# A spectral filter split into pieces between the steps of an FFN, forward and backward, in one kernel

## The chip, the cores and the metric

One core of a Trainium2 chip runs the whole program. The metric is the device time of one execution in microseconds (us). Ratios between kernels use runs that alternated on one chip. The kernel before has a median of 1678.64 us over the runs taken beside the changed one.

Names used below: PE multiplies matrices; PEld loads its weights; DVE, ACT and POOL are the vector, scalar and general-purpose engines; SP here only issues DMAs (its rows are marked SPq). L12 is line 12 of the kernel that the view is of.

## The reference, cut to what matters

The kernel computes a gated mix of a spectral filter and a GEGLU feed-forward network, and all seven gradients.

```python
def _A_ref(x, w_r, w_i):                      # x: 1 x 2048 x 576, bfloat16
    X = rfft2(x.astype(float32)) * (w_r + 1j * w_i)
    return irfft2(X, s=(S, D)).astype(bfloat16)

def _B_ref(x, w_gate, w_up, w_down):          # F = 4608
    return (gelu_tanh(x @ w_gate) * (x @ w_up)) @ w_down

g = sigmoid((x * gate_w).sum(-1, keepdims=True))
out = g * _A_ref(x) + (1 - g) * _B_ref(x)
# outputs: out, then by jax.vjp for grad_out: dx, dw_r, dw_i, dw_gate, dw_up, dw_down, dgate_w
```

## The kernel before

Five parts run one after another: setup (transposes of x, gate, sine and cosine tables); the spectral part as matmuls with those tables; the FFN's hidden layer in 18 groups of 8 steps, in which the last group's weight gradients are worked off between the steps of the next; and a final stage in two halves (down projection and gate, then dx), which reads the hidden activations back transposed by DMA.

The spectral part, one of its forward pieces. Of three evictions (`evac`) two go to ACT and one to DVE, from three PSUM buffers (`ps`):

```python
def fwd_D_S1_t(self, xT_t, t, scr):
    yps = self.ps.tile([P, 2, 512], F32, tag="specps")
    for c in range(2):
        for ci in range(5):
            nc.tensor.matmul(yps[:, c, :DF], lhsT=xT_t(ci), rhs=tb.Dfwd[:, ci, c, :], ...)
    Y = self.rot.tile([P, 2, DF], BF16, tag="specY")
    evac(nc, Y[:], yps[:, :, :DF])
    # ... four matmuls with R into vps, evac to V
    self.st.dma_start(scr[:, t, :, :], V[:])          # read back later with another layout
```

The gradient is scaled by 1 - g and transposed on PE:

```python
ident = res.tile([P, P], BF16, name="ident")
make_identity(nc, ident[:])                           # POOL
...                                                   # tables, whole spectral part
for t in range(T):
    # dB = don1 * omg32, DVE and ACT in turn
transpose_to_dchunks(nc, pst1, ident, lambda ci, t: dB[:, t, ...], dBT, T)
```

The FFN's step and its order:

```python
def H(g, tp):
    for w, xt in ((wg_g, xT), (wu_g, xT), (wdT_g, dBT)):
        # 10 matmuls of 256 columns into one PSUM bank
    # ... ACT: q, xb, hu, s (sigmoid), sq (square), da (copy);  DVE: 12 instructions
    for k, tl in enumerate((A, dHg, dHu)):
        LD.dma_start(scr[k][tp][:, :, fsl]..., tl[:])  # SP stores

for g in range(NG):                                    # 18
    for tp in range(NT):                               # 8
        H(g, tp)
        for _ in range(quota[tp]):
            if pend: pend.pop(0)()                     # weight-gradient work of group g-1
    pend = W_units(g)
```

The boundary to the final stage:

```python
for f0 in range(0, NFC, 12):
    LD.dma_start(wd_all[:, f0:f0 + 12, :], wd_v[:, f0:f0 + 12, :])
for u in pend: u()                                     # last weight gradients
...
ensure(6)                                              # first six transposed loads ("pin")
for t in range(T):                                     # first half: 72 matmuls of 288 columns per t
    ...
    if 1 <= t < 1 + len(wT_loads):                     # gate AND up weights, transposed, 12 loads
        LD.dma_start_transpose(...)
```

Of the kernel before, what the change touches and what calls it, by code (L numbers as in the profile page):

```python
# [9 lines left out]
ACT = mybir.ActivationFunctionType  # L10
# [18 lines left out]
A_GELU = 0.044715  # L29


def centered_mod(nc, pool, X, N, tagp=""):
    shp = list(X.shape)
    y = pool.tile(shp, F32, tag=tagp + "cm_y")
    nc.scalar.activation(y[:], X, ACT.Identity, scale=1.0 / N, bias=MAGIC)  # L35
    nc.scalar.activation(y[:], y[:], ACT.Identity, scale=1.0, bias=-MAGIC)  # L36
    r = pool.tile(shp, F32, tag=tagp + "cm_r")
    nc.vector.scalar_tensor_tensor(r[:], y[:], -float(N), X, op0=ALU.mult, op1=ALU.add)
    ar = pool.tile(shp, F32, tag=tagp + "cm_ar")
    nc.vector.scalar_tensor_tensor(ar[:], r[:], -1.0, r[:], op0=ALU.mult, op1=ALU.max)  # L40
    return r, ar


def trig(nc, r, ar, N, halfpi, cos_out=None, sin_out=None, nsin_out=None):
    s = 2.0 * math.pi / N
    if cos_out is not None:
        nc.scalar.activation(cos_out, ar, ACT.Sin, bias=halfpi, scale=-s)
    if sin_out is not None:
        nc.scalar.activation(sin_out, r, ACT.Sin, scale=s * EPS_SCALE)
    if nsin_out is not None:  # L50
        nc.scalar.activation(nsin_out, r, ACT.Sin, scale=-s * EPS_SCALE)
# [6 lines left out]
def build_tables(nc, tc, const_pool):  # L58
    tb = Tables()
    with tc.tile_pool(name="tbtmp", bufs=1) as tmp:  # L60
        halfpi = const_pool.tile([P, 1], F32, name="halfpi")
        nc.vector.memset(halfpi[:], math.pi / 2)
        tb.halfpi = halfpi
        lrow = tmp.tile([P, DF], F32, tag="lrow")
        nc.gpsimd.iota(lrow[:], pattern=[[1, DF]], base=0, channel_multiplier=0, allow_small_or_imprecise_dtypes=True)
        dcol = tmp.tile([P, 5], F32, tag="dcol")
        nc.gpsimd.iota(dcol[:, 0:4], pattern=[[128, 4]], base=0, channel_multiplier=1, allow_small_or_imprecise_dtypes=True)
        nc.gpsimd.iota(dcol[:, 4:5], pattern=[[0, 1]], base=DCH[4][0], channel_multiplier=1, allow_small_or_imprecise_dtypes=True)
        lcol = tmp.tile([P, 3], F32, tag="lcol")
        nc.gpsimd.iota(lcol[:, 0:2], pattern=[[128, 2]], base=0, channel_multiplier=1, allow_small_or_imprecise_dtypes=True)  # L70
        nc.gpsimd.iota(lcol[:, 2:3], pattern=[[0, 1]], base=LCH[2][0], channel_multiplier=1, allow_small_or_imprecise_dtypes=True)
        krow = tmp.tile([P, P], F32, tag="krow")
        nc.gpsimd.iota(krow[:], pattern=[[1, P]], base=0, channel_multiplier=0, allow_small_or_imprecise_dtypes=True)
        scol = tmp.tile([P, T], F32, tag="scol")
        nc.gpsimd.iota(scol[:], pattern=[[1, T]], base=0, channel_multiplier=16, allow_small_or_imprecise_dtypes=True)
        drow = tmp.tile([P, D], F32, tag="drow")
        nc.gpsimd.iota(drow[:], pattern=[[1, D]], base=0, channel_multiplier=0, allow_small_or_imprecise_dtypes=True)
        mrow_i = tmp.tile([P, P], I32, tag="mrow_i")
        nc.gpsimd.iota(mrow_i[:], pattern=[[1, P]], base=0, channel_multiplier=0)
        qcol_i = tmp.tile([P, 1], I32, tag="qcol_i")  # L80
        nc.gpsimd.iota(qcol_i[:], pattern=[[0, 1]], base=0, channel_multiplier=1)

        XD = tmp.tile([P, 5, DF], F32, tag="XD")
        for c in range(5):
            nc.vector.tensor_scalar(XD[:, c, :], lrow[:], dcol[:, c:c + 1], None, op0=ALU.mult)
        r, ar = centered_mod(nc, tmp, XD[:], D, "D")
        Dfwd = const_pool.tile([P, 5, 2, DF], BF16, name="Dfwd")
        trig(nc, r[:], ar[:], D, halfpi[:], cos_out=Dfwd[:, :, 0, :], nsin_out=Dfwd[:, :, 1, :])
        tb.Dfwd = Dfwd
        XR = tmp.tile([P, T, P], F32, tag="XR")  # L90
        for t in range(T):
            nc.vector.tensor_scalar(XR[:, t, :], krow[:], scol[:, t:t + 1], None, op0=ALU.mult)
        r, ar = centered_mod(nc, tmp, XR[:], S, "R")
        R = const_pool.tile([P, T, 3, P], BF16, name="Rtab")
        trig(nc, r[:], ar[:], S, halfpi[:], cos_out=R[:, :, 0, :], nsin_out=R[:, :, 1, :], sin_out=R[:, :, 2, :])
        tb.R = R
        k2row_i = tmp.tile([P, P], I32, tag="k2row_i")
        nc.vector.tensor_single_scalar(k2row_i[:], mrow_i[:], 3, op=ALU.arith_shift_right)
        jrow_i = tmp.tile([P, P], I32, tag="jrow_i")
        nc.vector.tensor_single_scalar(jrow_i[:], mrow_i[:], 7, op=ALU.bitwise_and)  # L100
        tcol_i = tmp.tile([P, 1], I32, tag="tcol_i")
        nc.vector.tensor_single_scalar(tcol_i[:], qcol_i[:], 3, op=ALU.arith_shift_right)
        jcol_i = tmp.tile([P, 1], I32, tag="jcol_i")
        nc.vector.tensor_single_scalar(jcol_i[:], qcol_i[:], 7, op=ALU.bitwise_and)
        k2row = tmp.tile([P, P], F32, tag="k2row")
        nc.vector.tensor_copy(k2row[:], k2row_i[:])
        jrow = tmp.tile([P, P], F32, tag="jrow")
        nc.vector.tensor_copy(jrow[:], jrow_i[:])
        tcol = tmp.tile([P, 1], F32, tag="tcol")
        nc.vector.tensor_copy(tcol[:], tcol_i[:])  # L110
        jcol = tmp.tile([P, 1], F32, tag="jcol")
        nc.vector.tensor_copy(jcol[:], jcol_i[:])
        XB = tmp.tile([P, P], F32, tag="XB")
        nc.vector.tensor_scalar(XB[:], k2row[:], tcol[:, 0:1], None, op0=ALU.mult)
        mask = tmp.tile([P, P], F32, tag="maskB")
        nc.vector.tensor_scalar(mask[:], jrow[:], jcol[:, 0:1], None, op0=ALU.is_equal)
        r, ar = centered_mod(nc, tmp, XB[:], 16, "B")
        Btmp = tmp.tile([P, 3, P], F32, tag="Btmp")
        trig(nc, r[:], ar[:], 16, halfpi[:], nsin_out=Btmp[:, 0, :], cos_out=Btmp[:, 1, :], sin_out=Btmp[:, 2, :])
        B = const_pool.tile([P, 3, P], BF16, name="Btab")  # L120
        for v in range(3):
            nc.vector.tensor_tensor(B[:, v, :], Btmp[:, v, :], mask[:], op=ALU.mult)
        tb.B = B
        XA = tmp.tile([P, 3, D], F32, tag="XA")
        for c in range(3):
            nc.vector.tensor_scalar(XA[:, c, :], drow[:], lcol[:, c:c + 1], None, op0=ALU.mult)
        r, ar = centered_mod(nc, tmp, XA[:], D, "A")
        Atmp = tmp.tile([P, 3, 2, D], F32, tag="Atmp")
        trig(nc, r[:], ar[:], D, halfpi[:], cos_out=Atmp[:, :, 0, :], nsin_out=Atmp[:, :, 1, :])
        clcol = tmp.tile([P, 3], F32, tag="clcol")  # L130
        sd = 1.0 / (S * D)
        m1 = tmp.tile([P, 3], F32, tag="m1")
        nc.vector.tensor_scalar(m1[:], lcol[:], 0.0, -sd, op0=ALU.is_equal, op1=ALU.mult)
        m2 = tmp.tile([P, 3], F32, tag="m2")
        nc.vector.tensor_scalar(m2[:], lcol[:], float(DF - 1), -sd, op0=ALU.is_equal, op1=ALU.mult)
        nc.vector.memset(clcol[:], 2.0 * sd)
        m3 = tmp.tile([P, 1], F32, tag="m3")
        nc.vector.tensor_scalar(m3[:], lcol[:, 2:3], 256.0, 2.0 * sd, op0=ALU.is_ge, op1=ALU.mult)
        nc.vector.tensor_copy(clcol[:, 2:3], m3[:])
        nc.vector.tensor_tensor(clcol[:], clcol[:], m1[:], op=ALU.add)  # L140
        nc.vector.tensor_tensor(clcol[:], clcol[:], m2[:], op=ALU.add)
        Ainv = const_pool.tile([P, 3, 2, D], BF16, name="Ainv")
        for c in range(3):
            nc.vector.tensor_scalar(Ainv[:, c, :, :], Atmp[:, c, :, :], clcol[:, c:c + 1], None, op0=ALU.mult)
        tb.Ainv = Ainv
        ucol = tmp.tile([P, 3], F32, tag="ucol")
        nc.vector.memset(ucol[:], 1.0)
        m4 = tmp.tile([P, 1], F32, tag="m4")
        nc.vector.tensor_scalar(m4[:], lcol[:, 2:3], 256.0, None, op0=ALU.is_ge)
        nc.vector.tensor_copy(ucol[:, 2:3], m4[:])  # L150
        Ainv_u = const_pool.tile([P, 3, 2, D], BF16, name="Ainv_u")
# [8 lines left out]
    return tb  # L160


_evac_ctr = [0]


def evac(nc, out, in_, eng=None):
# [595 lines left out]
```

## Time and profile before

| | before |
|---|---|
| time, median of 4 runs | 1678.64 us (1677.68 to 1680.4) |
| span of the profiled run, granted clock | 1676.1 us, 0.98 |
| first FFN step | 299 us |
| FFN after the first group, to the last weight gradient | 339.7 to 1206.9: 867 us |
| idle PE at the boundary | 5.6 us |
| final stage, halves | 170 and 293 us |

The page gives an engine's busy share first, and then tenths of busy time in 40 slices of 42 us:

```profile
PE 1540.7 (92%) x13440; PEld 1280.9 (76%) x13440; DVE 863.7 (52%) x2162; ACT 709.3 (42%) x1226; POOL 83.8 (5%) x171
...
PE   2777678899999999999999999999898889999998
PEclk9998888999999999999999999999999999999999
```

Eight slices at the left where PE is not full, then twenty where it is, then a final stage a little below. At the boundary SP's queue is short:

```profile
1184.36 6.09 SPq L614 DMA_DIRECT2D wd_all<-in_B_w_down_dram  x3
1190.56 6.25 SPq L563 DMA_DIRECT2D out_dram<-dwd  x2
...
1208.07 9.29 SPq L640 DMA_TRANSPOSE pin<-scr  x5
```

The columns are start, duration, engine, line, operation and count. The down weights are asked for at 1184, the stores of the last weight gradients follow, and the transposed loads start 1.2 us after PE has finished, at 1208.

### The profile page before, as it was taken

The page shows a single profiled execution, that of the slowest core. Times are in us where ns is not written, and L with a number is a line of the kernel's source. Part 1 is how long each engine was busy: PE and PEld are TensorE (multiplying, and loading weights), DVE is VectorE, ACT ScalarE, POOL GpSimd, SP SyncE. Part 2 cuts the span into 40 slices and gives each one's busy share as a digit, 9 for nine tenths or more (in the row PEclk, how much of TensorE's full clock was granted, in tenths as well). Part 3 has the DMA queues.
Part 4 walks back from the last instruction along what each step waited for, and adds up shares of the span by engine and source line. Part 5 has one row for each costly group of instructions (what it writes and reads, how often), then busy time and mean ns, then how long its engine had stood idle before and what let it go on. Part 6 is the DMA issues. An engine that isn't in the chain of part 4 may idle for free.

```text
span 1676.1 us, 33316 instructions
## 1 busy us (share of the span) xinstructions
PE 1540.7 (92%) x13440; PEld 1280.9 (76%) x13440; DVE 863.7 (52%) x2162; ACT 709.3 (42%) x1226; POOL 83.8 (5%) x171
## 2 busy tenths in 40 slices
PE   2777678899999999999999999999898889999998
PEld 2554455788888888888888888888776667777776
DVE  6127520787777777777777777777222221001001
ACT  7554446666665556565556565556100000000000
POOL 1122231000000000000000000000000000000000
PEclk9998888999999999999999999999999999999999
DMA  3244564243332443432343342333699998877773
GB/s 117 103 110 114 152 173 134 61 120 104 105 102 83 109 108 105 108 98 84 104 109 107 109 101 85 101 106 86 201 207 226 210 214 170 157 147 154 151 150 85
DMA packets 490395, 212.42 MB, mean 127 GB/s; under 512 B 306560, under 2 KB 484608, under 8 KB 489728
## 3 DMA queue, kind: packets, MB, share of 16 engines
q1 hardware_dynamic: 483424, 189.01, 49.1%
q0 software_dynamic: 6816, 21.28, 3.7%
q8 instruction: 105, 1.72, 0.4%
q14 instruction: 50, 0.41, 0.1%
HBM read 43.25 MB, written 93.82 MB: 82 GB/s over the span
## 4 chain that ended last, share of the span: by engine, by line
issue 87%; PE 6%; ACT 2%; POOL 2%; DMA 1%; DVE 1%; SPq 0%; POOLq 0%; ACTq 0%
PE yps L202 2%; PE yps L269 1%; ACT Y L171 1%; DMA wg_g<-in_B_w_gate_dram 1%; POOL scr_p L246 1%; POOL out_dram L685 1%; POOL dxa_scr L282 1%; DMA xn<-in_A_x_dram 0%; POOL out_dram L731 0%; PE vps L208 0%; PE zps L254 0%; SPq L221 0%; PE zps L256 0%; ACT y L36 0%; ACT y L35 0%
## 5 line engine op out<-in xcount | busy, mean ns | idle before, releaser
L502 PEld LDWEIGHTS <-xT 128*128 128x128 bf16 x2880 | 281.8, 98 | 42.6 <-issue 8.7
L718 PEld LDWEIGHTS <-pin 128*128 128x128 bf16 x2304 | 225.4, 98 | 56.8
L571 PEld LDWEIGHTS <-xn 128*128 128x128 bf16 x2304 | 224.0, 98 | 29.7 <-issue 3.6
L502 PE MATMUL hps<-wu_g,xT 128*128 128x256 bf16 x1440 | 180.7, 273 | 7.1 <-ACT da L520 7.0
L502 PE MATMUL hps<-wg_g,xT 128*128 128x256 bf16 x1440 | 180.7, 273 | 0.4 <-ACT dBT L171 0.4
L502 PE MATMUL hps<-wdT_g,dBT 128*128 128x256 bf16 x1440 | 180.7, 273 | 0.0
L672 PE MATMUL bps<-wd_all,pin 128*128 128x288 bf16 x1152 | 151.2, 296 | 24.7 <-DMA pin<-scr 24.7
L672 PEld LDWEIGHTS <-pin 128*128 128x128 bf16 x1152 | 115.5, 101 | 60.4 <-DMA pin<-scr 28.0
L502 PEld LDWEIGHTS <-dBT 128*128 128x128 bf16 x1440 | 140.9, 98 | 16.3
L555 PE MATMUL wps<-dB,A 128*128 128x288 bf16 x1152 | 152.4, 286 | 0.0
L511 ACT ACTIVATE q<-hps 128x512 bf16<-128x512 f32 x144 | 86.1, 598 | 153.8 <-PE hps L502 152.4
L718 PE MATMUL xps<-wgT_all,pin 128*128 128x288 bf16 x1152 | 149.0, 286 | 0.0
L718 PE MATMUL xps<-wuT_all,pin 128*128 128x288 bf16 x1152 | 149.0, 286 | 0.0
L728 DVE SCALAR_TENSOR_TENSOR f32t<-gwf,dlog,f32t 128x576 f32<-128x576 f32 x16 | 13.1, 817 | 240.5 <-ACT f32t L726 240.5
L555 PEld LDWEIGHTS <-A 128*128 128x128 bf16 x1152 | 112.7, 98 | 26.6
L571 PE MATMUL wps<-dHu,xn 128*128 128x256 bf16 x1152 | 131.7, 273 | 0.0
L571 PE MATMUL wps<-dHg,xn 128*128 128x256 bf16 x1152 | 131.5, 273 | 0.0
L518 ACT ACTIVATE s<-s 128x512 bf16<-128x512 bf16 x144 | 90.9, 631 | 92.0 <-DVE s L514 92.0
L726 ACT COPY f32t<-xps 128x576 f32<-128x576 f32 x16 | 10.2, 640 | 275.9 <-PE xps L718 275.9
L519 ACT ACTIVATE sq<-s,nhalf 128x512 bf16<-128x512 bf16 x144 | 104.0, 722 | 4.7
L513 DVE TENSOR_SCALAR s<-q 128x512 bf16<-128x512 bf16 x144 | 41.6, 289 | 113.9 <-ACT q L511 113.9
L517 ACT CAST hu<-hps 128x512 bf16<-128x512 f32 x144 | 84.7, 588 | 2.1
(200 smaller groups left out, 1885.0 us busy)
## 6 DMA issues: line engine op xcount, KB each, us to landing
scr<-A SPq DMA_DIRECT2D x144, 128.0 KB, 1.8
scr<-dHg SPq DMA_DIRECT2D x144, 128.0 KB, 1.9
scr<-dHu SPq DMA_DIRECT2D x144, 128.0 KB, 1.9
out_dram<-dw SPq DMA_DIRECT2D x72, 128.0 KB, 1.8
out_dram<-dwd SPq DMA_DIRECT2D x36, 144.0 KB, 1.9
wd_all<-in_B_w_down_dram SPq DMA_DIRECT2D x3, 1728.0 KB, 13.2
scr_p<-V POOLq DMA_DIRECT2D x32, 144.5 KB, 2.5
Vp<-scr_p SPq DMA_DIRECT2D x16, 289.0 KB, 7.1
```

The lines of the kernel that those rows point to most:

```text
L171: nc.scalar.copy(out, in_)
L202: nc.tensor.matmul(yps[:, c, :DF], lhsT=xT_t(ci), rhs=tb.Dfwd[:, ci, c, :], start=(ci == 0), stop=(ci == 4))
L502: nc.tensor.matmul(pt[:, tt, :], lhsT=xt[:, ci, tp * TPB + tt, :], rhs=w[:, ci, :], start=(ci == 0), stop=(ci == 4))
L511: nc.scalar.activation(q[:], hg[:], ACT.Square)
L513: V.tensor_scalar(s[:], q[:], A_GELU, 1.0, op0=ALU.mult, op1=ALU.add)
L517: nc.scalar.copy(hu[:], hu_ps[:])
L518: nc.scalar.activation(s[:], s[:], ACT.Sigmoid, scale=2.0 * C_GELU)
L519: nc.scalar.activation(sq[:], s[:], ACT.Square, bias=nhalf[:])
L555: nc.tensor.matmul(wps[:, :288], lhsT=tl(0, t)[:, fch * P:(fch + 1) * P], rhs=dB[:, t, h * 288:(h + 1) * 288], start=(t == 0), stop=(t == ...
L571: nc.tensor.matmul(wps[:, cc, :], lhsT=xn[:, t, (c0 + cc) * P:(c0 + cc + 1) * P], rhs=tl(k, t), start=(t == 0), stop=(t == T - 1))
L672: nc.tensor.matmul(bps[:, h, :288], lhsT=At[:, r, :], rhs=wd_all[:, fc, h * 288:(h + 1) * 288], start=(fc == 0), stop=(fc == NFC - 1))
L718: nc.tensor.matmul(xps[:, h, :288], lhsT=src[:, r, :], rhs=wT[:, fc, h * 288:(h + 1) * 288], start=(n < 2), stop=(n >= 4 * NFC - 2))
```

## The change

Its intent is to fill PE from the start: the spectral part no longer runs ahead of the FFN but is cut into 192 pieces (201 slots, with gaps), which are emitted between the FFN's steps; every order is set by hand. To reach the FFN sooner, the gradient is transposed by DMA instead of by PE, and the scaling by 1 - g moves behind the matmul (`da`). The transposed gate weights become a loop of 18 loads ahead of the final stage. ACT loses two instructions of a step and gains a second sigmoid; DVE takes over the eviction of `da`. To make room, the FFN's buffers shrink: its steps get 4 PSUM banks instead of 5, its weight gradients 2 instead of 3, and its element-wise and staging tiles two buffers instead of three.

```diff
-        with tc.tile_pool(name="pA", bufs=1) as pA, ...:      # the whole spectral part, 4 phases
-            ...
+    for t in range(T):
+        load_dOT(t)                       # two DMA transposes on SP, straight from DRAM
+        if t % 4 == 3:
+            nc.gpsimd.memset(dOT[0:D4NEW, 4, t - 3:t + 1, :], 0.0)
+            LD.dma_start(dB[:, t - 3:t + 1, :], do_v[:, t - 3:t + 1, :])
+    ...
+    ident = res.tile([P, P], BF16, name="ident")
+    make_identity(nc, ident[:])
+    tb = iotas(nc, res, unit)             # POOL
     ...
-        nc.scalar.activation(sq[:], s[:], ACT.Square, bias=nhalf[:])
-        nc.scalar.copy(da[:], da_ps[:])
+        nc.scalar.activation(om[:], s[:], ACT.Sigmoid, scale=-2.0 * C_GELU)
+        V.tensor_tensor(da[:], da_ps[:], omg32[:, t0:t0 + TPB].unsqueeze(2).to_broadcast([P, TPB, FG]), op=ALU.mult)
     ...
+    def pftile():
+        return pf.tile([P, 2, 512], F32, tag="pf", name="pf")   # one buffer of two banks
+    ...                                   # forward, middle and inverse pieces, all evicted by ACT
+        for p in range(T // 2):           # middle
+            if p > 0:
+                out.append(pre(p))        # loads Vp (two), Wt (two) for this pair
+            out += [s2(p, "x", 0), s2(p, "x", 1), s2(p, "g", 0), s2(p, "g", 1)]
+            ...
+            out += [s1(p, "m1", 0, scr_p1), s1(p, "m1", 1, scr_p1)]
     for g in range(NG):
         for tp in range(NT):
-            H(g, tp)
+            fft_until(want(step, 0))      # pieces that are due
+            pts = H_mm(g, tp)
+            tiles = H_ew1(g, tp, pts)
+            fft_until(want(step, 1))
+            H_ew2(g, tp, tiles)
             ...
+    wgT_all = []
+    for f0 in range(0, NFC, 2):
+        u = unit([2, D], name="wgT")
+        LD.dma_start_transpose(u[:], B_w_gate[:, f0 * P:(f0 + 2) * P])
     wd_all = ...                          # loads, weight gradients, final stage as before
```

## The prediction

> **What bounds the kernel now.** I first cut the run at the program's own stages with the view of busy time by stretch, cuts from the order-of-time view: spectral part and setup, first FFN group (18 groups of 8 steps), other groups, last weight-gradient work, and the two halves of the final stage.
>
> ```profile
> 0.00:298.90 298.90, 202.45 (x1600) 147.58 (x1601) 115.41 (x206) 163.40 (x249) 65.94 (x138) 0.93 0.44 127
> 298.90:339.70 40.80, 33.67 (x300) 29.27 (x300) 35.17 (x98) 27.87 (x51) 0.00 (x0) 1.00 0.26 72
> 339.70:1183.00 843.30, 843.30 (x7831) 739.77 (x7830) 635.25 (x1709) 495.24 (x889) 0.00 (x0) 1.00 0.38 101
> 1183.00:1211.70 28.70, 23.91 (x226) 20.24 (x223) 3.46 (x7) 2.34 (x5) 0.00 (x0) 0.96 0.80 247
> 1211.70:1382.60 170.90, 150.97 (x1152) 115.51 (x1153) 44.33 (x105) 9.59 (x15) 8.14 (x15) 0.95 1.13 213
> 1382.60:1676.00 293.40, 286.43 (x2339) 228.56 (x2336) 30.10 (x41) 10.88 (x17) 9.76 (x18) 1.00 0.75 145
> ```
>
> Columns: stretch, length, busy us of PE, weight load, DVE, ACT, POOL, then granted clock, DMA share, GB/s. From 340 to 1183 PE never idles at clock 1.00, DVE 75%, ACT 59%. In the first 299 us no engine is full: a chain of stages. From 1212 to 1383 the DMA share is over 1. The list of waits says what PE waited for:
>
> ```profile
> PE bps L672 <- DMA pin<-scr: 24.7, 11, 5.6
> PE zps L254 <- DMA wg_g<-in_B_w_gate_dram: 13.1, 1, 13.1
> PE vps L208 <- ACT Y L171: 12.1, 18, 0.8
> PE tp L184 <- ACT xT L171: 11.9, 4, 9.5
> PE zps L254 <- DMA Vp<-scr_p: 11.6, 1, 11.6
> ```
>
> The first is the final stage's transposed loads; the rest are spectral. Busy PE overstates: the starts in order of time give PE's true pace.
>
> ```profile
> 602.10 1.25 PE L502 MATMUL hps<-wg_g,xT 128*128 128x256 bf16 x10
> 603.19 1.25 PE L502 MATMUL hps<-wu_g,xT 128*128 128x256 bf16 x10
> 604.28 1.25 PE L502 MATMUL hps<-wdT_g,dBT 128*128 128x256 bf16 x10
> 605.38 2.12 PE L555 MATMUL wps<-dB,A 128*128 128x288 bf16 x16
> 607.34 3.66 PE L571 MATMUL wps<-dHg,xn 128*128 128x256 bf16 x32
> 610.83 1.25 PE L502 MATMUL hps<-wg_g,xT 128*128 128x256 bf16 x10
> ```
>
> A step's 30 matmuls take 3.28 us (109 ns each at 256 columns), a dwd piece 1.96 (122.5 ns at 288), a dw piece 3.49. A group is 8x3.28 + 4x1.96 + 4x3.49 + 1.9 (tail) = 49.9 us, without a gap.
>
> **What the Trainium skill says.** "VectorE: DVE Perf Modes", The perf-mode tier table: tensor_tensor runs 2x from bf16 SBUF and 1x with a PSUM operand. The trace agrees (groups by shape, FFN stretch and, last, spectral stretch; the numbers after the bar are total us and ns of one):
>
> ```profile
> L514 DVE TENSOR_TENSOR s<-xb,s 128x512 bf16<-128x512 bf16 x127 | 54.0, 425 | 18.4 <-ACT xb L512 11.7
> ...
> L513 DVE TENSOR_SCALAR s<-q 128x512 bf16<-128x512 bf16 x127 | 36.7, 289 | 105.8 <-ACT q L511 105.8
> ...
> L234 DVE TENSOR_TENSOR Gspec<-xps,srow 128x578 bf16<-128x578 f32 x16 | 11.3, 753 | 1.0 <-PE xps L230 1.0
> ```
>
> "DMA: Bandwidth & Descriptors", DMA Transpose (X-bar): the plain DMA transpose comes from Sync or Scalar only; so the new ones lengthen SP's queue, where each cost 1.2 to 1.9 us of issue in this trace. Same page, Two DMAs through the same engine are not ordered: a DMA reading what another wrote must wait for its completion; Vp loads after scr stores show it (11.6 us above). "TensorE: Matmul & The Clock Gate", opening table: DVE and ACT are strict FIFO, so spectral pieces placed behind FFN work wait for it. This trace's fixed order is consistent, but does not isolate it.
>
> **The change part by part.** Times are from the span's start.
>
> (1) Removed: the separate spectral stage, 298.9 us. What must remain on PE is its matmuls: forward 32x(10+4) and middle 64x4 at 124 ns, inverse 32x(6 at 109 + 12 at 122.5 ns) = 55.7 + 32 + 67.8 = 155 us. They enter a PE without gaps, so all but some 6 us in the first group's gaps are paid: 150.
>
> (2) New setup. DVE now builds all tables in small float32 pieces before the first step. With this trace's durations (0.48 per 128x289 scaling, 150 + n/0.96 ns for the scalar-tensor form, 0.2 to 0.5 otherwise): D 9, x's evictions 3.4, R 13.5, B 4, A 9, started at 3.5, so 43; sigmoid and table load 3; 16 dB scalings 5. On SP, 32 gradient transposes at about 1.2 (wdT's small ones take 1.22 to 1.29) are 39 after 10 us of loads; the last dB load lands near 53. Both agree: the first step's DVE work starts at 54, not 299.
>
> (3) First group, DVE-bound before (35.2 of 40.8). DVE per step after: 9 tensor_tensor x 0.425 + 3 tensor_scalar x 0.287 + da from PSUM 0.69 (753 scaled to 512) = 5.4; queued instructions overlap about 6% (the same sum before gives 40.0 per group against 37.5 busy), so 5.06. Eight make 40.5: group done at 94.5.
>
> (4) Groups to the end of weight gradients: before 1211.7 - 339.7 = 872, PE-paced, unchanged. Plus 150.
>
> (5) Stalls from interleaving. Program order, which I counted, puts 201 slots (192 pieces) on 135 steps. DVE per group: 8x5.06 plus evictions 1.6 = 42 of 60 us: fine in the forward and inverse part. In the middle (5.6 groups) products add per pair 6x0.76 + 6x0.46 + 0.3 = 7.6 us, 1.49 pairs per group, so 52.5 of 56 us. There DVE paces the first four steps of a group (6.5 us against PE's 5.7), and each pair's Vp load is issued immediately before its use, behind the previous step's stores. A step's DVE work ends about 7.4 to 8 us after its first matmul, plus issue and landing about 3 = 10.9. The eight first uses fall where PE arrives at about 10, 11, 5.7, 3.8, 11, 5.2, 6.6, 11: waits 1+1+6+7+1+6+4+1 = 27. With product waits 6 and DVE pacing elsewhere 7: 40. The single two-bank PSUM buffer costs about 0.7 at each group with no weight work between two pieces: 5.
>
> (6) Final stage. 5.3 MB of gate-weight transposes leave the DMA-bound half (36.6 MB in 171 us, 213 GB/s): 31.3 MB takes 147, near PE's 1152x0.1225 = 141, so 146. But they now precede wd_all and the first pin loads on SP: 18 at about 1.6 = 29 us, then wd_all issue 6, output stores 5, pin 2 + 4.3 landing = 46, against 28 us of remaining weight work: a new wait of 17. Second half unchanged: 293.4.
>
> Sum: 94.5 + 872 + 150 + 45 + 17 + 146 + 293 = 1617.5; add 1.8 of time over span: 1619. Shares of (5) and (6) may hide in each other's slack, and an ordering this deliberate suggests fewer waits than worst case; I lower it by 9: **1610 us**, 4% faster.
>
> **Rivals.**
> A, nearly all waits vanish: PE is in order but DVE catches up in heavy weight-work steps, and SP runs ahead. For it: no PE wait in 843 us now. Then (5) is about 10 and (6) about 5: about 1565.
> B, DVE becomes the bound: if broadcast products miss the 2x rate they take 1.35 us, DVE needs about 58 of 56 us in the middle, and every Vt and Y eviction sits behind a sigmoid that waits for DVE. Against: the present odd-offset products already take 0.76. It would give 1650.
> C, DMA contention and SP's blocking order delay weight loads: FFN DMA share is 0.38 and the spectral traffic adds little; against, except at the boundary. Time 1630 to 1650.
>
> **Range and chances.** A and B bracket the range: 1560 to 1655. Two per cent is 1645; only B or C in full reach it. Faster 0.83, same 0.15, slower 0.02.
>
> **What would show it.** Right: first FFN step's DVE work near 54; a PE without gaps in forward and inverse groups, its length near 60 us per group; in the middle groups PE waits on Vp loads and products of 30 to 45 us in all; DVE near 94% there; a wait of 10 to 20 us between the last weight gradient and the first bps matmul; bps half near 146. Wrong: a first step after 65, PE waits spread over all groups, DVE full outside the middle, product instructions near 1.35 us, or no wait at the boundary.

## The result, and the profile after

The changed kernel is correct and slower: 1730.95 us (1728.73 to 1733.01, 4 runs) against 1678.64 us. The ratio is 1.031, 95% interval 1.0292 to 1.0328. A ratio is the mean time of one kernel's runs over that of the other's of the same rounds, so it isn't quite the ratio of the medians. The profiled run's span is 1729.0 us at clock 0.962.

The page of after, to set against the one of before:

```profile
PE 1519.5 (88%) x13280; PEld 1275.0 (74%) x13280; DVE 907.1 (52%) x2295; ACT 624.3 (36%) x1093; POOL 25.7 (1%) x55
...
PE   0339999999987797898999999999929999999998
PEclk9869999999998999999999999999969999999999
```

Three holes appear: nothing on PE in the first slice and little in the next two; dips to 7 and 8 between the 12th slice and the 19th; and a slice at 2 of 10 near the end. The view of busy time by stretch, cut at the stages of after (columns as in the prediction), gives their lengths:

```profile
0.00:57.70 57.70, 0.00 (x0) 0.10 (x1) 0.06 (x1) 1.28 (x1) 2.76 (x11) 1.00 0.55 138
57.70:109.80 52.10, 19.45 (x220) 17.38 (x220) 42.95 (x109) 24.08 (x43) 4.99 (x12) 0.67 0.13 30
109.80:161.20 51.40, 40.43 (x316) 32.90 (x316) 44.35 (x122) 30.76 (x55) 0.00 (x0) 0.90 0.27 75
161.20:455.90 294.70, 293.04 (x2664) 252.59 (x2662) 200.54 (x523) 158.44 (x281) 0.00 (x0) 1.00 0.37 100
455.90:830.00 374.10, 318.69 (x2776) 268.49 (x2775) 277.95 (x706) 179.06 (x319) 0.00 (x0) 0.94 0.42 113
...
1256.00:1290.50 34.50, 0.00 (x1) 0.01 (x1) 1.06 (x2) 0.58 (x1) 0.00 (x0) 0.55 0.93 246
1290.50:1435.90 145.40, 143.23 (x1153) 113.24 (x1154) 44.88 (x105) 9.57 (x15) 8.26 (x15) 0.99 1.14 215
1435.90:1729.00 293.10, 286.30 (x2338) 228.45 (x2335) 30.10 (x41) 10.85 (x17) 9.72 (x18) 1.00 0.73 144
```

The first 57.7 us hold almost nothing on any engine. The forward groups (161 to 456) are full, as the prediction has it. In the middle (456 to 830) DVE is at 278 of 374 us, 74%, and PE is not full either: nobody is the bound, they wait. Then comes a hole of 34.5 us. Both halves of the final stage are what was predicted.

The list of PE's waits (line, what for, total us, times, longest):

```profile
PE tp L259 <- POOL ident masks.py:199: 57.7, 1, 57.7
PE pf L475 <- DMA Vp<-scr_x: 44.4, 8, 11.4
PE acc L739 <- DMA pin<-scr: 36.7, 4, 34.5
...
PE pf L412 <- ACT Y L416: 6.0, 1, 6.0
```

**The first hole.** POOL, in order of time; the bracket gives the idle time before and what ended it:

```profile
23.87 0.52 POOL L232 MEMSET dOT<- 64x512 bf16 x1 [23.41 <-DMA dOT<-in_grad_out_dram]
34.94 0.52 POOL L232 MEMSET dOT<- 64x512 bf16 x1 [10.56 <-DMA dOT<-in_grad_out_dram]
46.07 0.52 POOL L232 MEMSET dOT<- 64x512 bf16 x1 [10.62 <-DMA dOT<-in_grad_out_dram]
56.63 0.52 POOL L232 MEMSET dOT<- 64x512 bf16 x1 [10.04 <-DMA dOT<-in_grad_out_dram]
57.09 0.20 POOL masks.py:197 MEMSET ident<- 128x128 bf16 x1
...
57.79 0.39 POOL L76 IOTA lrow<- 128x289 f32 x1
```

Each memset clears the unused half of the last chunk of four row tiles, whose DMA transposes stand just ahead of it in the program, so it waits for them to land. The identity and the index rows need nothing and take about 3 us (57.09 to 59.91), but they were emitted later and stand behind the fourth memset. DVE's tables follow them:

```profile
58.22 1.17 DVE L112 TENSOR_SCALAR XD<-lrow,dcol 128x289 f32<-128x289 f32 x2 [57.34 <-POOL lrow L76]
...
105.37 4.56 DVE L646 TENSOR_SCALAR dB<-dB,omg 128x576 bf16<-128x576 bf16 x16
109.84 0.28 DVE L306 TENSOR_SCALAR s<-q 128x512 bf16<-128x512 bf16 x1
```

The tables run from 58.2 to 101.8, and the first FFN step's DVE work starts at 109.84.

**The first group.** The first piece's matmuls start at 120.28; the second piece waits for their eviction by ACT. First PE and then ACT, in order of time:

```profile
120.28 1.40 PE L412 MATMUL pf<-Dt,xT 128*128 128x289 bf16 x10
127.68 2.58 PE L412 MATMUL pf<-Dt,xT 128*128 128x289 bf16 x10 [5.99 <-ACT Y L416]
```

```profile
120.77 0.63 ACT L311 ACTIVATE om<-s 128x512 bf16<-128x512 bf16 x1 [2.30 <-DVE s L307]
...
125.81 0.63 ACT L311 ACTIVATE om<-s 128x512 bf16<-128x512 bf16 x1 [2.30 <-DVE s L307]
126.47 0.63 ACT L312 ACTIVATE s<-s 128x512 bf16<-128x512 bf16 x1
127.00 0.62 ACT L416 CAST Y<-pf 128x578 bf16<-128x578 f32 x1
```

ACT is idle for 2.3 us twice, waiting for DVE's input of a sigmoid, and the eviction stands behind both sigmoids. There is one buffer, so PE stops for 6 us. The ten matmuls then take 2.58 us instead of 1.40: the granted clock is 0.50 from 127.6 to 133.0.

**The dips.** SP around the third pair, then PE:

```profile
544.54 0.42 SPq L332 DMA_DIRECT2D scr<-dHu  x1
545.94 0.37 SPq L521 DMA_DIRECT2D out_dram<-o  x1
...
546.92 0.45 SPq L445 DMA_DIRECT2D Vp<-scr_x  x1
```

```profile
538.50 2.12 PE L356 MATMUL wps<-dB,A 128*128 128x288 bf16 x16
550.88 0.42 PE L475 MATMUL pf<-Vp,Btab 128*128 128x289 bf16 x1 [10.26 <-DMA Vp<-scr_x]
...
551.82 2.34 PE L293 MATMUL hps<-wg_g,xT 128*128 128x256 bf16 x10
553.96 2.34 PE L293 MATMUL hps<-wu_g,xT 128*128 128x256 bf16 x10
```

The load of `Vp` is issued at 546.92, behind the stores of the step before, which wait for DVE; PE has been ready since 540.6. After the wait, two sets of ten matmuls take 2.34 us each instead of the usual 1.25: another 2 us per wait.

**The boundary.** SP after 1233, and the first matmul of the final stage:

```profile
1233.70 30.50 SPq L676 DMA_TRANSPOSE wgT<-in_B_w_gate_dram  x18
1264.29 7.45 SPq L682 DMA_DIRECT2D wd_all<-in_B_w_down_dram  x3
1271.84 5.64 SPq L364 DMA_DIRECT2D out_dram<-dwd  x2
...
1286.13 11.68 SPq L707 DMA_TRANSPOSE pin<-scr  x6
```

The gate transposes hold SP for 30.5 us, everything behind them starts that much later, and the loads that PE needs come at 1286, against 1208 before, where no gate transposes stood in front.

### The profile page after: what moved, and what is told of

Read it like the earlier page. It is cut to its first block, busy times and chain, and to the rows that moved or that the text cites. A ratio compares the mean times of both kernels' runs of the same rounds, so it can differ in the third digit from the quotient of the medians.

```text
span 1729.0 us, 32828 instructions
## 1 busy us (share of the span) xinstructions
PE 1519.5 (88%) x13280; PEld 1275.0 (74%) x13280; DVE 907.1 (52%) x2295; ACT 624.3 (36%) x1093; POOL 25.7 (1%) x55
## 4 chain that ended last, share of the span: by engine, by line
PE 64%; issue 15%; DVE 9%; SPq 4%; DMA 4%; ACT 2%; POOL 0%; POOLq 0%; ACTq 0%; DVEq 0%
PE hps L293 22%; PE wps L372 14%; PE wps L356 7%; PE acc L739 7%; PE pf L601 3%; PE pf L412 2%; PE acc L786 2%; PE wps L383 2%; DMA Vp<-scr_x 2%; SPq L225 1%; DMA pin<-scr 1%; SPq L226 1%; DVE s L307 1%; PE pf L585 1%; PE pf L587 1%
## 5 line engine op out<-in xcount | busy, mean ns | idle before, releaser
L786 PEld LDWEIGHTS <-pin 128*128 128x128 bf16 x2304 | 225.4, 98 | 56.8
L293 PE MATMUL hps<-wu_g,xT 128*128 128x256 bf16 x1440 | 186.6, 278 | 24.6 <-ACT xb L305 24.6
L293 PE MATMUL hps<-wg_g,xT 128*128 128x256 bf16 x1440 | 186.2, 278 | 2.2 <-DVE da L314 2.2
L293 PE MATMUL hps<-wdT_g,dOT 128*128 128x256 bf16 x1440 | 182.3, 274 | 0.0
L739 PE MATMUL acc<-wd_all,pin 128*128 128x288 bf16 x1152 | 143.4, 288 | 36.7 <-DMA pin<-scr 36.7
L293 PEld LDWEIGHTS <-dOT 128*128 128x128 bf16 x1440 | 142.0, 99 | 17.5
L786 PE MATMUL acc<-wuT_all,pin 128*128 128x288 bf16 x1152 | 149.0, 286 | 0.0
L786 PE MATMUL acc<-wgT,pin 128*128 128x288 bf16 x1152 | 149.0, 286 | 0.0
L794 ACT COPY f32t<-acc 128x576 f32<-128x576 f32 x16 | 10.2, 638 | 275.9 <-PE acc L786 275.9
L311 ACT ACTIVATE om<-s 128x512 bf16<-128x512 bf16 x144 | 91.0, 632 | 48.8 <-DVE s L307 48.7
L314 DVE TENSOR_TENSOR da<-hps,omg 128x512 bf16<-128x512 f32 x144 | 99.3, 689 | 3.9 <-PE hps L293 3.9
```

The lines of the kernel that those rows point to most:

```text
L293: nc.tensor.matmul(pt[:, tt, :], lhsT=xt[:, ci, tp * TPB + tt, :], rhs=w[:, ci, :], start=(ci == 0), stop=(ci == 4))
L311: nc.scalar.activation(om[:], s[:], ACT.Sigmoid, scale=-2.0 * C_GELU)
L314: V.tensor_tensor(da[:], da_ps[:], omg32[:, t0:t0 + TPB].unsqueeze(2).to_broadcast([P, TPB, FG]), op=ALU.mult)
L739: nc.tensor.matmul(bps[:, h, :288], lhsT=At[:, r, :], rhs=wd_all[:, fc, h * 288:(h + 1) * 288], start=(fc == 0), stop=(fc == NFC - 1))
L786: nc.tensor.matmul(xps[:, h, :288], lhsT=src[:, r, :], rhs=wT[:, h * 288:(h + 1) * 288], start=(n < 2), stop=(n >= 4 * NFC - 2))
```

## The experiments

The first five experiments edit the changed kernel (1730.95 us); those after the three cures build on the version with all cures. Times are medians of four runs (five for the last), each beside the kernel before, which took 1680.14, 1679.68 and 1683.35 us on the chips of the three sets. Differences in us from the changed kernel are of medians of the first two sets, and good to the 1.5 us by which the kernel before differed there. The third set fell on a slower chip, so its kernels are compared by their ratios to the kernel before.

The theories at the start: Q, POOL's order makes the first hole; V, the place of the load makes the dips; B, the bytes and the queue of the gate transposes make the third. The rivals were that the DMA transposes themselves set the start, that DVE's load sets the middle, and that plain order on SP sets the boundary.

### Identity and index rows first on POOL

```diff
+    ident = res.tile([P, P], BF16, name="ident")
+    make_identity(nc, ident[:])
+    tb = iotas(nc, res, unit)
+    nc.gpsimd.memset(xT[0:D4NEW, 4, :, :], 0.0)
     wts = {0: load_w(0)}
     ...                                    # DMA transposes and their memsets
-    (the same four lines)
```

> Changed kernel (1730.95) with the identity, the iotas and the clearing of xT moved in the program ahead of the loop that loads the transposed gradient; nothing else. Theory Q (POOL's fixed order: its four memsets of the transposed gradient wait for 32 transposing loads, and the identity and iotas stand behind them): the first FFN step's DVE work moves from 109.8 to about 60 us, now set by the last load of the gradient, issued at 55 and landing near 59; time about 1682. Rival R (the setup is long because the tables are many small pieces on DVE, 43 us of work, whenever they begin, or SP's 39 us of transposes alone set it): no more than 10 us are gained, about 1721 to 1730.

Measured: 1683.99 us (1682.28 to 1685.5), ratio 1.0026 (1.0011 to 1.0041); 47.0 us less than the changed kernel. Nothing but the order of POOL's work was touched, so the first hole is POOL's order. What sets the first step now is the last load of the gradient's plain copy, which is issued behind the transposes:

```profile
60.94 1.21 DVE L646 TENSOR_SCALAR dB<-dB,omg 128x576 bf16<-128x576 bf16 x4 [9.60 <-DMA dB<-in_grad_out_dram]
62.07 0.28 DVE L306 TENSOR_SCALAR s<-q 128x512 bf16<-128x512 bf16 x1
```

### The middle's loads two pieces earlier

```diff
         for p in range(T // 2):
-            if p > 0:
-                out.append(pre(p))
             out += [s2(p, "x", 0), s2(p, "x", 1), s2(p, "g", 0), s2(p, "g", 1)]
             ...
+            if p + 1 < T // 2:
+                out.append(pre(p + 1))
             out += [s1(p, "m1", 0, scr_p1), s1(p, "m1", 1, scr_p1)]
```

> Changed kernel with the three loads of each middle pair issued two pieces earlier, before the last two pieces of the pair before. Theory V (each pair's first matmul waits for a load that is issued only when it is needed, 44.4 us in eight waits, and PE then runs at a lower granted clock for some us): waits on the load below 12 us and the clock near 1.00 in the middle stretch; about 1685. Rival D (DVE is nearly full there and would set the pace anyway): the wait moves to products and evictions, time within 12 us of 1731.

Measured: 1684.45 us (1683.52 to 1685.49), ratio 1.0029 (1.0014 to 1.0044); 46.5 us less. The wait for `Vp` falls from 44.4 to 1.9 us, and the middle stretch from 374.1 to 334.1:

```profile
PE pf L475 <- DMA Vp<-scr_x: 1.9, 2, 1.4
...
455.90:790.00 334.10, 314.61 (x2848) 270.39 (x2848) 282.24 (x720) 180.90 (x324) 0.00 (x0) 1.00 0.46 129
```

DVE does the same work in less time (84% busy), so it wasn't what held the middle. The clock is back at 1.00 from 0.94, and PE's busy time from the first weight gradient to the last falls from 1030.1 to 1018.9 us: about 11 us of the loss were matmuls at a low clock, not idle time. Some 7 us come back at the same matmuls (L475), as waits for ACT's evictions of the piece before.

### Gate transposes in the last six steps

```diff
+            if step >= NG * NT - 6:
+                load_wgT(3)               # three of the 18 loads, behind each step's stores
-    for f0 in range(0, NFC, 2):           # the loop ahead of the down weights goes
```

> Changed kernel with the 18 gate-weight transposes spread over the last six FFN steps, three a step, where the DMA share is below 0.5, instead of after the last step. Theory B (the 34.5 us without any matmul at the boundary are the 30.5 us of these transposes in SP's queue ahead of the down weights, the stores and the first inputs): the gap falls to under 6 us and the time to about 1700. Rival S (the slots of the shared pool are not free, or the queue is then late for the weight loads and stores of the last steps): the gap stays or PE waits inside the last group; about 1720 to 1735.

Measured: 1708.3 us (1707.16 to 1710.53), ratio 1.0173 (1.0158 to 1.0188); 22.6 us less, not the hoped 31. The gap shrinks to 12.4 us rather than to before's 5.6. The list of waits has:

```profile
PE acc L746 <- DMA pin<-scr: 13.7, 3, 12.4
```

### Gate transposes in the final stage's first half, as before

```diff
-    for f0 in range(0, NFC, 2):
-        ...
+            if t >= 1:
+                load_wgT(2)               # two loads per tile of the first half
```

> Changed kernel with the same 18 transposes put into the down-projection half, two after each tile, so that they are only reordered, not moved to an idle stretch. If the order in SP's queue alone makes the gap: gap under 6 us, half unchanged at 145 us, time about 1700. If the bytes are the bound there (42 MB at 213 GB/s are 197 us, from 1234 on): the gap goes, the half grows from 145 to about 172 us as in the kernel before, time about 1725.

Measured: 1727.9 us (1726.92 to 1730.2), ratio 1.0291 (1.0274 to 1.0308): about 3 us gained. The gap is back at 5.6 us, but the half takes 171 us again instead of 145. So it's not only a matter of order: where DMA is full (share 1.13 in this half), moving 5.3 MB into it costs what moving it out saved.

### The gradient transposed by PE again

```diff
-        load_dOT(t)
+    for sN, dT in ((xn, xT), (dB, dOT)):  # PE transposes from the plain copy
         ...
```

> Changed kernel with one part undone: the gradient is transposed by PE again (80 transposes through PSUM, ten evictions shared by DVE and ACT) from the copy that is loaded anyway; the order of POOL's instructions is left as it was. Theory Q: POOL's memsets then wait for nothing, so the tables start near 4 us; tables 43, sigmoid 3.5, scalings 5, and five more evictions on DVE 3.5: first step's DVE work near 56 instead of 110, time about 1677, as good as moving the identity. Rival: the transposing loads are only harmful through SP's queue time, and POOL is a detail; then the two cures (this one and the moved identity) would differ by the 39 us of SP's transposes, this one near 1645 or lower.

Measured: 1681.27 us (1680.64 to 1681.98), ratio 1.001 (0.9989 to 1.0031); 49.7 us less. POOL's order is that of the changed kernel, but its memsets wait for no DMA any more and end at 2.7 us, and the first step starts at 59.3:

```profile
0.75 1.90 POOL L231 MEMSET dOT<- 64x512 bf16 x4 [0.29 <-POOLq L814]
```

```profile
59.31 0.29 DVE L306 TENSOR_SCALAR s<-q 128x512 bf16<-128x512 bf16 x1
```

With the first run this settles the cause: either taking the wait off the memset or taking the rest from behind it brings the 47 to 50 us back. The DMA transpose was harmful through the memset behind it. What it is worth without that shows in the next run, where the first step starts at about 53.5, 6 us earlier.

### The three cures together

The first three edits in one kernel, and the four loads of the gradient's plain copy moved ahead of the transposes:

```diff
     wts = {0: load_w(0)}
+    for t in range(0, T, 4):
+        LD.dma_start(dB[:, t:t + 4, :], do_v[:, t:t + 4, :])
     for t in range(T):
         load_dOT(t)
```

> All cures together: identity and iotas first, the gradient's plain loads ahead of its transposing ones, middle loads two pieces earlier, gate-weight transposes in the last six steps. If the losses are separate stretches, they add: 1731 - 47 (identity) - 46 (middle loads) - 23 (gate weights) - about 9 for the plain loads going first (first DVE step near 52 instead of 62) = 1606. If they share slack, some of it comes back: above 1625. Either way faster than both kernels by over 2 per cent.

Measured: 1606.1 us (1604.77 to 1609.46), ratio 0.9566 (0.9543 to 0.9588), correct: 4.3% faster than the kernel before, and near the 1610 of the prediction. That nearness is luck: the prediction held 27 us of waits for `Vp` and a gap of 22.6, which the cures took to 2 and 11.8, and in return had the first group 11 us too short and took 9 us off its sum. The gains add: 47.0 + 46.5 + 22.6 and 8.6 for the first step (62.07 to about 53.5) make 124.7, against 124.9 measured.

### Without the spectral pieces

The list of pieces is emptied and the scratch tensors are filled with x, so that the FFN's three weight gradients stay right and the output, dx, dw_r, dw_i and dgate_w are wrong.

```diff
-    fft = fx + fg + [gap] * 3 + mid_units() + ...
+    fft = []
```

> The three-cures kernel with all 192 spectral pieces left out, the tables still built (wrong in all outputs that need them on purpose; plain copies stand in for them). Theory P (PE is paid for the pieces in full and nearly nothing else): it is faster than the three-cures kernel by the 150 to 155 us of spectral matmuls plus the evictions' waits still left, 160 to 170 in all. Rival H (pieces partly hide in PE's gaps): less than 140.

Measured: 1418.59 us (1418.39 to 1420.63), ratio 0.8449 (0.8431 to 0.8467). The pieces cost 187.5 us in the cured kernel, though their matmuls are 155. They're not hidden at all, and some 33 us of waiting come with them: the first group takes 51.9 us with them and 42.0 without; from there to the last weight gradient it's 1048.5 against 871. The expectation was 20 us too low.

### Three staging buffers instead of two

```diff
-    stage = wstack.enter_context(tc.tile_pool(name="stage", bufs=2))
+    stage = wstack.enter_context(tc.tile_pool(name="stage", bufs=3))
```

> The three-cures kernel with three staging buffers for the weight gradients' stores instead of two, as in the kernel before. With the gate weights in the last steps there were still 12.4 us before the first input of the last stage, and SP stood 5.6 us for the last two stores, whose evictions wait for a staging buffer. If that is what holds the first inputs: gap 5 to 7 us, time 5 to 6 us below the three-cures kernel. If the down weights' 5.3 MB set it: no change.

Measured: 1606.44 us (1604.37 to 1609.71), ratio 0.956 (0.9534 to 0.9587): no change, and a gap of 12.7 us. The wait of the last evictions for a staging buffer, which the trace of the cured kernel shows, was a symptom: with three buffers it is gone, but the last two stores then hold SP for 5.35 us instead of 0.90. The theory that forecast 5 to 6 us of gain missed.

### Pieces from step 8 on

```diff
-    START, LAST = 3, NG * NT - 6
+    START, LAST = 8, NG * NT - 6
```

> The version with the three cures, with the spectral pieces starting at step 8 instead of step 3, so that the first group holds none (it held eight pieces, about 7 us of matmuls). Lock-step theory (the first group is slow because each new spectral piece waits for ACT to evict the one before from the single buffer, behind sigmoids that wait for DVE): the first group falls from 51.9 to about 42 us as in the run without spectral pieces, the first weight-gradient matmul moves from 105.4 to about 95.5; the eight pieces are paid later, where PE has no gaps, so the time falls by only about 3, to 1603. Rival, the clock: the first group is slow because PE idles at a low clock and not because of the pieces: the first weight-gradient matmul stays later than 102 and the time rises by up to 7, to 1613.

Measured: 1623.95 us (1622.97 to 1627.16), ratio 0.9652 (0.9638 to 0.9665), so 0.9% slower than the cured kernel. Both theories missed the time; of the clock's, the later first weight-gradient matmul came true, but not its reason. The trace shows eight steps at DVE's pace, from the third on at the full rate of 1.25 us for ten matmuls, then the same stop at the first pair of pieces, only later:

```profile
80.70 1.25 PE L294 MATMUL hps<-wg_g,xT 128*128 128x256 bf16 x10 [1.60 <-DVE da L315]
...
89.02 1.40 PE L413 MATMUL pf<-Dt,xT 128*128 128x289 bf16 x10
96.42 2.58 PE L413 MATMUL pf<-Dt,xT 128*128 128x289 bf16 x10 [6.00 <-ACT Y L417]
```

The first weight-gradient matmul comes at 102.9 instead of 105.4, not at 95.5. From there to the last one it takes 1065.6 us instead of 1048.5: about 7 us are the eight pieces that had run in the first group, 7 are longer waits (36.5 us in all against 29.4; one load of `Vp` in the inverse part alone is waited for 8.2 us against 4.2), and some 3 stay unexplained. So the stop belongs to the first meeting of the pieces with a DVE-bound step, and moving all pieces changes where loads and uses fall.

### The down weights split

```diff
-    for f0 in range(0, NFC, 12):
-        LD.dma_start(wd_all[:, f0:f0 + 12, :], wd_v[:, f0:f0 + 12, :])
+    LD.dma_start(wd_all[:, 0:12, :], wd_v[:, 0:12, :])
     ...                                   # last weight gradients
+        ensure(3)
+        LD.dma_start(wd_all[:, 12:24, :], wd_v[:, 12:24, :])
+        ensure(4)
+        LD.dma_start(wd_all[:, 24:36, :], wd_v[:, 24:36, :])
         ensure(6)
```

> The version with the three cures, with only the first third of the down weights loaded ahead of the last weight-gradient stores, and the other two thirds behind the first three and four transposed loads of the final stage. Bandwidth theory (the 5.3 MB of down weights fill the DMA engines for 15 us, so the last stores of weight gradients, and with them the staging buffers and the memory that the final stage's first loads take, come free late): the gap at the boundary falls from 11.8 to about 6, the time from 1606 to about 1600. Rival, issue order (the transposed loads' own issue and landing, about 5 us after the last eviction, set the gap): the gap stays within 2 us of 11.8 and the time within 2 of 1606.

Measured: 1611.73 us (1608.91 to 1612.14), ratio 0.9572 (0.9559 to 0.9585), the same as the cured kernel's 0.9566. The first wait halves as the bandwidth theory has it, and the rest comes back 24 matmuls later:

```profile
1162.40 5.85 PE L750 MATMUL acc<-wd_all,pin 128*128 128x288 bf16 x24 [5.82 <-DMA pin<-scr]
1172.81 5.76 PE L750 MATMUL acc<-wd_all,pin 128*128 128x288 bf16 x24 [4.55 <-DMA wd_all<-in_B_w_down_dram]
```

The gap was therefore set by the down weights standing in front of the stores, and yet splitting them gains nothing, since the next of them are needed 6 us later. The time's half of the expectation failed; the gap's half held.

### The late start and the split together

> Both edits on the version with the three cures: 1597 if both theories hold and the gains add, 1603 to 1613 if neither does.

Measured: 1625.97 us (1624.08 to 1626.94), ratio 0.9659 (0.9645 to 0.9672), as the late start alone, and outside both ranges expected. The cured kernel remains the best of all that ran.

## Why the prediction was wrong, by its own steps

The predicted terms against the spans of the changed kernel:

| step of the prediction | predicted | measured | difference |
|---|---|---|---|
| (2) first step's DVE work starts | 54 | 109.8 | +55.8 |
| (3) first group | 40.5 | 51.4 | +10.9 |
| (4), (5) to the last weight gradient | 867 + 150 + 45 = 1062 | 1094.8 | +32.8 |
| (6) gap (before's 5.6 + new 17) | 22.6 | 34.5 | +11.9 |
| first half | 146 | 145.4 | -0.6 |
| second half | 293.4 | 293.1 | -0.3 |

The prediction's 872 held before's gap; here it is split into 867 and 5.6. The predicted column sums to 1618.5, the differences to 110.5, together the span of 1729.0. The prediction had then taken 9 us off, for an ordering that looked deliberate; no view of the profile supported that.

**(2) is the step that failed most: half the error.** "Both agree: the first step's DVE work starts at 54." Of its two chains the tables were right in size, 43 us (58.2 to 101.8). The loads were a little low: the transposes took 1.21 to 1.27 us each, but the last gradient load was issued only at 55.4, not landed at 53. With POOL's order cured the first step came at 62.1, so some 8 of the 55.8 us belong to this. The other 48 come from the claim that the two chains run side by side. The prediction said the tables "started at 3.5"; it never asked what stood in front of the index rows on POOL. The program order shows it: four memsets, each behind DMA transposes. So 58 and 43 us, and then 8 for the sigmoid and the scalings, came one after the other. The prediction quoted the Trainium skill for DVE and ACT as strict FIFO ("TensorE: Matmul & The Clock Gate", opening table), and that same line names GpSimdE too; the trace of after agrees, with 3 us of ready POOL work held for 57 us. Emitting that work first was worth 47.0 us in its own experiment.

**(3) failed by 11 us.** DVE's pace of 5.06 per step was right: eight steps started 5.04 to 5.07 apart in the late-start run, and without pieces the first group takes 42.0. The failing claim stands in (1), that pieces in the first group use PE's gaps. In that group ACT waits for DVE, the eviction waits behind ACT's sigmoids, and one buffer passes that on to PE. This chain is read from the trace. The late start shows the same 6 us where its first pair falls, at step 8. The prediction gave the single buffer 5 us over the whole run, and looked for its cost at groups without weight work, not at this one.

**(4) and (5) failed by 33 us.** The mechanism in (5) was right: PE waits for `Vp` at the eight first uses, behind the stores. The eight waits were 1.3, 5.2, 10.3, 8.0, 2.2, 11.4, 3.8 and 2.2 us where the prediction had 1, 1, 6, 7, 1, 6, 4 and 1. So nearly every one was longer, by up to 5.4 us, and they sum to 44.4 instead of 27. PE waits in this stretch sum to 64.8 us, 20 more than the 45, and 11 us came from a term that the sum didn't have: after the longer waits the matmuls ran at a low clock (2.34 us for ten, not 1.25). Some 2 us are left over. The third part, "DVE near 94%" in the middle, was wrong as well: 74% over the stretch, 84% once the loads came early. The 7 us for DVE's pace didn't show as such. Outside the first group (1) held, that the pieces' matmuls are paid and not hidden: in the cured kernel the pieces cost 187.5 us, their 155 and some 33 of waits, which in the prediction stand under (3) and (5).

**(6) was right in kind and low by 12 us.** The first half came to 145.4 and the second to 293.1, both within 1 us. The new wait was there, 28.9 us over before's gap, against 17. The transposes took 30.5 us (predicted 29) and the down weights' issue 7.45 (predicted 6). But then the sum was 46: the trace has 52.4 from 1233.7 to the first transposed load at 1286.1, and 4.4 of landing, 56.8 in all. The term that was low is the output stores: 14.3 us (1271.8 to 1286.1) instead of 5, of which SP issues nothing from 1280.2 to 1285.1, where the last evictions wait for earlier stores to free the staging buffers. In the cured kernel a third buffer only moved that wait, and splitting the down weights ahead of the stores halved the gap. The PE work beside it was as expected, 22.3 us (1233.7 to 1256.0): the prediction's 28 is before's stretch from 1183 to 1211.7, in which PE worked 24 us and stood for most of before's gap.

Two slips in the prediction's sums are small: in (5), 42 and 1.49 times 7.6 make 53.3, not 52.5; in (6), 46 less 28 is 18, not 17.

The rivals: A needed waits to vanish, and no part of it came. B is refuted by DVE's shares; the broadcast products took 0.756 us and not 1.35, as this row of the groups shows:

```profile
L504 DVE TENSOR_TENSOR n<-Xg,Wt 128x1156 bf16<-128x1156 bf16 x16 | 12.1, 756 | 0.0
```

Of C, the blocking order on SP is what happened in the middle and at the boundary, beyond the share that (5) and (6) had counted of it; but it held up `Vp` and the final stage's loads, and the list of waits has none for the weight loads that C names. None of the three touched the first 110 us, though the prediction's own sign, "a first step after 65", pointed there. The range of 1560 to 1655 was too narrow for that reason: it varied the waits already listed and left no room for one that wasn't.

What stays open: why the `Vp` waits were longer than worked out (their parts weren't measured one by one); some 3 us of the late start's loss; whether a second buffer, or evictions on another engine, would end the stop of the first group, which no run tries; what the smaller buffers cost, of which only the staging ones were tested; and whether anything lowers the boundary's cost in the cured kernel, which two edits failed to move.

## What to carry to other kernels

When the order is set by hand, read the program order of every engine, POOL and SP included, and ask of each instruction what stands in front of it: an instruction that waits for a DMA holds everything behind it, however small and ready. Emit loads a piece or two before their use, ahead of the stores that wait for compute; price a wait of 10 us on PE at 2 us more, for the clock. And before calling a change bad, take out its faults one at a time: this one was 3.1% slower as written and 4.3% faster with four reorderings.

## What the Trainium skill lacked or had wrong

- "TensorE: Matmul & The Clock Gate", opening table, lists the strict FIFO for ScalarE, VectorE and GpSimdE and is right. What it lacks is the consequence: in this trace 3 us of ready POOL work (identity and index rows) was held for 57 us by four memsets that waited for DMAs, and cost 47.0 us of time.
- The same page, Part 1: The HAM clock gate, has the half clock after idle and about 3.4 us to return. The half agrees: after a wait of 10.26 us the granted clock was 0.50, and ten matmuls of 256 columns took 2.34 us against 1.25. The return took longer here: 5.3 us of work at 0.50 (550.8 to 556.1), and 5.4 in the first group (127.6 to 133.0). The page says the ramp penalty is under 1% of a typical span, and that holds: the eight waits on loads left PE 11 us more of busy time than the same stretch had without them, 0.6% of the span.
- "DMA: Bandwidth & Descriptors" gives a bandwidth for transposing loads, but for their time in the issuing queue only a count of sequencer cycles on "previous generations", in a section on trn3, and no time measured on this chip. Here one held SP for 1.21 to 1.27 us, the same for four chunks of the gradient and for one, and 1.7 us (30.5 us for 18) with the larger gate loads.
- The same page, Latency and other measured facts, has 261 GB/s for transposing loads, measured on one kernel. Here it was less: while SP issued nothing but the 18 gate transposes (1234 to 1264), 173 GB/s at a DMA share of 1.00; and in the first half of the final stage, with transposed loads and some plain ones, 214 GB/s at 1.13 when it was DMA-bound.
